# Loading keys' weight in four pieces and x tile by tile, with a new order of work, in a linear-attention block

## The chip, the cores and the metric

The kernel runs on one core of a Trainium2 chip. The metric is the device time of one execution in microseconds. Three runs of the kernel before took 169.29, 169.65 and 170.04 us; the median is 169.65.

## The reference

x has 2048 rows of 512 numbers in bf16. The block is a pre-normalized linear attention with 32 heads of 16 columns, followed by a pre-normalized dense layer with 1792 hidden columns, each with a residual:

```python
qkv = layernorm(x) @ wqkv                       # q, k, v: 32 heads of 16
phi = lambda t: where(t > 0, t + 1, exp(t)) + 1e-6
kv  = einsum("bhsd,bhse->bhde", phi(k), v)
z   = einsum("bhsd->bhd", phi(k))
o   = (phi(q) @ kv) / (phi(q) . z + 1e-6)
h   = x + o @ wo
out = h + relu(layernorm(h) @ w1) @ w2
```

## The kernel before

The 2048 rows are 16 tiles of 128 rows, and four chunks of four tiles. The program holds no loop over the work: a list of words, `ORDER` (line 18), is read from left to right (lines 539 to 542), and each word calls one small function with the numbers that follow it. The order of the words is the order of each engine's own queue. Nothing else plans the work. Each engine runs its queue in order, and an instruction waits for the data and the buffers that it needs. The landing of a DMA is signalled on one of eight semaphores, which the DMAs of both queues take in turn (the prediction calls them marks); the issue of a DMA whose semaphore is in use waits on its queue until the DMA eight places before it has landed.

The words that matter here, in the order of the computation of one tile `t`:

- `lx.t.n` loads `n` tiles of x from tile `t` on SyncE's queue (line 213), `ax.t.n` the same on ScalarE's queue (line 216). A group of `n` tiles puts `n` neighbouring rows into one partition (`rows_of`, line 101), and the output is written with the same grouping. `lk`, `lq`, `lv`, `lo`, `l1` and `l2` load pieces of the weights on SyncE's queue through `load_d` (line 219); the first number is the block of 128 rows, the second the count of blocks.
- `table` loads ScalarE's function table (line 177). `const` and `masks` fill constants on DVE and POOL. `warm` runs matmuls on zeros on PE (line 230).
- `S.t` and `A.t` are the mean and variance of a tile on DVE (lines 233 and 234), `R.t.n` the inverse root on ScalarE, an Ln and an Exp (lines 239 and 240), `N.t` the normalization on DVE (line 247). `N.t.k.n` does only `n` of the four blocks of columns.
- `T.t.b` transposes the tile on PE into bank `b` (line 272), and `E.t` copies it to SBUF on ScalarE (line 282). `X.t` transposes by a DMA on SyncE's queue instead (line 293). Both give `lnT`, the input of the products. Tiles 0 to 4 go through PE, the others through the DMA.
- `K.t.b` is the product with keys' weight, four matmuls of 512 columns, into bank `b` (line 301); `K.t.b.k.n` does only `n` of the four. `Q.c.j.b` is the product with queries' weight for a chunk (line 309).
- `F` and `U` are an exp and a relu on ScalarE, `M` and `D` a minimum and an add on DVE; together they are phi. `qF`, `qU`, `qM` and `qD` are the same for queries.
- `G.t` collects phi(k) times the normalized tile in banks 4 to 7 on PE (line 353); `gA` and `gD` copy the result on ScalarE and DVE. `z*`, `kv`, `kx`, `m`, `mA` and `mD` make the small matrices of the attention from it.
- `d4`, `dl4`, `dx4` give the reciprocal of the denominator; `wb` writes it to DRAM and `rb` (eight of them for a chunk, line 456) reads it back repeated over the columns of a head; `dm` multiplies it into phi(q) (line 469).
- `h.t.b` is the attention's output product (line 478), `hD` adds x, `s`, `a`, `r`, `n` or `nA` normalize again, and `t` with `v`, or the DMA transpose `x`, turn the tile.
- `p.c.f.b` is the first dense product (line 493; `ph` is half of it, line 502), with `pA` on ScalarE or `pD` on DVE for the relu (lines 509 and 513). `f.t.b` is the second dense product (line 522), `fo` scales and adds on DVE (line 530), into one of four output buffers (tile modulo four), and `fd` stores it (line 537).

PSUM has eight banks. A product that writes a bank waits until the instruction that reads the bank's former content is done.

The loads stand at the head of the list. ScalarE issues tiles 1 and 2 and then loads its table. SyncE issues tile 0, the whole of keys' weight, tile 3, tiles 4 and 5, tiles 6 and 7, queries' weight, tiles 8 to 11 and tiles 12 to 15. Tile 0 is normalized, transposed and copied in two halves. The output's buffers `o_t` are those of `gT`, so a store shows as `gT` in the profile, and `x_nat` is x.

Of the kernel before, what the change touches and what calls it, by code (L numbers as in the profile page):

```python
# [23 lines left out]
K.5.7 M.3.1 A.12 A.8 A.9 S.13 S.11 qU.0.0.2 X.6 qF.0.0.2 Q.0.2.0 D.2.1 A.11 K.6.2 A.13 X.7 U.4.2 F.4.2 R.8.2
qM.0.0.2 D.3.1 K.7.3 N.9 M.4.2 N.8 D.4.2 S.14 R.12.2 R.10.2 N.13 A.14 S.15 qF.0.2.2 X.9 N.10 A.15 G.0 G.2 G.1
N.12 G.3 G.4 G.5 X.8 F.6.2 U.6.2 X.13 K.9.3 R.14.2 qU.0.2.2 K.8.2 N.11 M.6.2 qD.0.0.2 D.6.2 N.15 N.14 F.8.2
U.8.2 K.13.1 X.12 X.11 qM.0.2.2 K.12.0 za.4.1 M.8.2 F.12.2 U.12.2 X.10 qD.0.2.2 G.7 K.11.3 X.14 K.10.2 G.6 D.8.2
za.6.0 X.15 K.14.0 F.10.2 M.12.2 lv.2.2 U.10.2 K.15.1 za.8.0 M.10.2 G.9 lv.0.2 zf D.10.2 G.8 zhi D.12.2 F.14.2
G.10 M.14.2 zlo G.12 U.14.2 D.14.2 z.3.3 z.0.3 z.1.3 z.2.3 zc zh G.14 d4.0.3 G.11 G.15 G.13 dl4.0 dx4.0 lo.0.2
gA.0.2 Q.1.1.3 Q.1.0.2 qF.1.0.2 lo.2.2 gD.2.2 kv.1.7 kv.2.7 kv.3.7 kv.0.7 qU.1.0.2 Q.1.3.1 qM.1.0.2 kx qD.1.0.2  # L30
Q.1.2.0 l1.0.2 m.3.7 m.2.6 mD.2.2 wb.0 rb.0.7 rb.0.3 rb.0.0 rb.0.6 rb.0.4 qF.1.2.2 qU.1.2.2 qM.1.2.2 Q.2.1.5
m.1.3 m.0.2 mA.0.2 rb.0.1 rb.0.2 Q.2.0.4 Q.2.3.1 Q.2.2.0 qF.2.0.2 qU.2.0.2 qD.1.2.2 rb.0.5 dm.0.2.2 dm.0.0.2
h.1.6 l1.2.2 d4.1.5 qF.2.2.2 qM.2.0.2 h.0.4 hD.1 dl4.1 s.1 dx4.1 a.1 hD.0 nA.1 s.0 a.0 n.0 Q.3.0.2 l2.0.7 h.2.5
hD.2 s.2 qU.2.2.2 Q.3.1.3 qU.3.0.2 wb.1 x.1 h.3.7 a.2 Q.3.3.6 hD.3 qF.3.0.2 n.2 Q.3.2.5 t.2.0 x.0 ph.0.3.1.0 s.3
a.3 n.3 ph.0.1.3.0 t.3.7 ph.0.0.2.0 rb.1.1 v.2 qM.2.2.2 r.0.4 rb.1.2 rb.1.5 qF.3.2.2 v.3 qM.3.0.2 qM.3.2.2
ph.0.2.0.0 ph.0.2.0.1 rb.1.7 ph.0.3.1.1 qD.2.0.2 qD.3.0.2 ph.0.0.2.1 qU.3.2.2 qD.3.2.2 qD.2.2.2 ph.0.1.3.1
p.0.9.5 p.0.8.4 pA.0.2.2 rb.1.3 rb.1.4 rb.1.6 d4.2.6.2 rb.1.0 dm.1.0.2 l2.7.7 dm.1.2.2 h.4.1 pD.0.0.2 dl4.2
dl4.3 dx4.2 wb.2 rb.2.6 hD.4 s.4 h.5.6 h.7.7 rb.2.7 hD.5 h.6.0 a.4 rb.2.0 rb.2.3 rb.2.4 pA.0.8.2 hD.7 hD.6 s.5
s.6 p.0.7.6 a.5 rb.2.1 p.0.6.5 p.0.4.2 p.0.5.3 s.7 a.6 a.7 p.0.13.1 rb.2.2 rb.2.5 n.4 n.7 n.5 n.6 pD.0.4.2
pD.0.6.2 p.0.11.4 p.0.12.0 dm.2.2.2 dm.2.0.2 dx4.3 p.0.10.3 pD.0.10.2 pD.0.12.2 wb.3 rb.3.4 f.2.6.0.7 rb.3.0  # L40
h.10.5 hD.10 x.6 h.9.4 hD.9 rb.3.2 rb.3.7 h.8.2 s.10 hD.8 a.10 h.11.0 s.9 s.8 rb.3.1 rb.3.6 rb.3.5 rb.3.3 hD.11
a.9 a.8 s.11 n.8 a.11 n.9 f.2.6.7.7 x.7 f.1.7.0.7 f.0.2.0.7 f.0.2.7.7 dm.3.0.2 n.10 n.11 dm.3.2.2 fo.2 fo.0
h.15.3 hD.15 x.5 x.4 x.11 h.12.4 h.13.0 s.15 hD.12 h.14.2 hD.13 a.15 s.12 f.3.3.0.7 x.10 r.4.4 p.1.0.1 hD.14
a.12 s.13 x.9 r.8.4 f.3.3.7.7 s.14 a.13 a.14 p.1.11.6 n.13 n.14 n.15 p.1.10.5 x.8 n.12 fo.3 pD.1.10.2 p.1.1.2
pD.1.0.2 f.1.7.7.7 fd.3 r.12.4 fo.1 p.1.6.3 fd.1 x.14 fd.2 p.1.7.4 p.1.3.1 p.1.4.6 p.1.5.7 p.1.2.0 pD.1.6.2
p.1.13.3 p.1.12.2 pD.1.4.2 pD.1.2.2 x.15 fd.0 x.12 pD.1.12.2 p.2.8.5 p.2.9.6 p.2.6.3 p.2.7.4 p.1.8.1 p.1.9.2
pD.2.8.2 pD.2.6.2 p.2.10.4 p.2.11.5 pD.1.8.2 pD.2.10.2 f.7.6.0.7 f.7.6.7.7 fo.7 p.2.0.4 p.2.1.5 f.4.0.0.7
f.4.0.7.7 x.13 pD.2.0.2 fo.4 f.6.1.0.7 fd.7 f.6.1.7.7 fo.6 f.5.3.0.7 f.5.3.7.7 p.3.4.5 p.3.5.6 fo.5 p.3.11.4
p.3.10.3 p.3.9.1 p.3.8.0 pD.3.4.2 p.3.6.5 p.3.7.6 pD.3.10.2 pD.3.8.2 pD.3.6.2 p.3.0.2 p.3.1.3 pD.3.0.2 p.3.3.1
p.3.2.0 pD.3.2.2 p.3.12.5 p.3.13.6 fd.4 fd.6 p.2.5.3 pD.3.12.2 f.15.4.0.14.3.1 fo.15.3.1 f.15.5.0.14.0.2  # L50
fo.15.0.2 fd.5 p.2.4.2 pD.2.4.2 p.2.3.1 p.2.2.0 p.2.12.6 pD.2.2.2 p.2.13.7 pD.2.12.2 f.8.1.0.7 f.8.1.7.7 fo.8
fd.8 f.12.4.0.7 f.12.4.7.7 fo.12 f.10.7.0.7 f.10.7.7.7 fo.10 f.13.6.0.7 fd.12 fd.10 fd.15.0.2 f.13.6.7.7 fo.13
fd.15.3.1 f.11.0.0.7 f.11.0.7.7 fo.11 fd.13 fd.11 f.14.3.0.7 f.14.3.7.7 fo.14 fd.14 f.9.0.0.7 f.9.0.7.7 fo.9
# [5 lines left out]
def kernel(  # L59
# [157 lines left out]

    def load_d(dst, src, k, n):
        nc.sync.dma_start(out=dst[:, k : k + n, :], in_=src[:, k : k + n, :])
# [353 lines left out]
```

## Time and profile before

| | |
|---|---|
| median of three runs | 169.65 us |
| profiled execution | 169.61 us |
| its span, from the first to the last instruction | 167.9 us |
| PE busy | 162.2 us |
| DVE busy | 115.8 us |
| ScalarE (ACT) busy | 49.9 us |
| bytes moved by DMA | 16.01 MB |

The profile is one execution. Times in it count from the start of the span. A row of the timeline or of the chain gives the start, the duration, the engine, the line of the kernel and the operation, `xN` for N neighbours that are merged; square brackets give the idle time before it and what ended that. PE is the matrix unit, PEld its weight loads, DVE VectorE, ACT ScalarE, POOL GpSimd, SPq and ACTq the issue of a DMA from SyncE's and ScalarE's queue. A merged row of matmuls lasts a little longer than its share of the stream, since matmuls overlap; the chain's rows give the stream.

### The profile page before, as it was taken

How to read it: one execution, taken by the hardware profiler on the slowest of the kernel's cores; microseconds unless marked ns; L12 is line 12 of the kernel's file. 1: busy time of each engine (PE TensorE's matmuls, PEld its weight loads, DVE VectorE, ACT ScalarE, POOL GpSimd, SP SyncE). 2: the span in 40 equal slices, each digit the busy share in tenths (PEclk: the TensorE clock that was granted, in tenths of full speed). 3: DMA queues.
4: the chain of work that ended last, by engine and by line, in shares of the span. 5: the costliest groups of instructions: out<-in, count | busy, mean ns of one | idle time of the engine just before them, and what ended most of it. 6: DMA issues, size and time to landing. Idle time of an engine off the chain costs nothing.

```text
span 167.9 us, 2399 instructions
## 1 busy us (share of the span) xinstructions
PE 162.2 (97%) x908; PEld 79.5 (47%) x924; DVE 115.8 (69%) x218; ACT 49.9 (30%) x84; POOL 4.7 (3%) x21
## 2 busy tenths in 40 slices
PE   7899999999999999999999999999999999999992
...
PEclk9999999999999999999999999999999999999999
...
GB/s 147 372 234 96 18 106 95 186 315 37 131 341 157 106 228 72 147 43 118 106 94 31 31 89 132 2 0 31 31 66 0 0 0 0 0 66 55 31 62 39
DMA packets 25003, 16.01 MB, mean 95 GB/s; under 512 B 15008, under 2 KB 23968, under 8 KB 24992
## 3 DMA queue, kind: packets, MB, share of 16 engines
...
q8 instruction: 7, 0.11, 0.3%
...
## 4 chain that ended last, share of the span: by engine, by line
PE 93%; DVE 2%; DMA 2%; issue 1%
PE bk L522 29%; PE bk L493 26%; PE bk L478 8%; PE bk L301 8%; PE bk L353 8%; PE bk L309 8%; PE bk L502 2%; DMA x_nat<-in_A_x_dram 2%; DVE st L233 1%; PE bk L272 1%; PE bk L425 1%; DVE gT L530 1%; PE bk L377 1%; PE bk L399 1%; PE bk L411 1%
## 5 line engine op out<-in xcount | busy, mean ns | idle before, releaser
L522 PE MATMUL bk<-w_sb,at 128*128 128x512 bf16 (+2 forms) x250 | 49.8, 355 | 0.2
L493 PE MATMUL bk<-lnT,w_sb 128*128 128x512 bf16 x200 | 45.5, 379 | 0.3
L513 DVE TENSOR_SCALAR at<-bk 128x1024 bf16<-128x1024 f32 x26 | 31.4, 1222 | 11.8 <-PE bk L493 9.4
L522 PEld LDWEIGHTS <-at 128*128 128x128 bf16 x252 | 23.6, 98 | 25.4
L493 PEld LDWEIGHTS <-w_sb 128*128 128x128 bf16 x208 | 20.3, 98 | 24.1
L530 DVE SCALAR_TENSOR_TENSOR gT<-bk,rstd,h_nat 128x512 bf16<-128x512 f32 (+2 forms) x18 | 12.4, 691 | 25.5 <-PE bk L522 25.2
L319 ACT ACTIVATE eb<-bk 128x1024 bf16<-128x1024 f32 (+1 forms) x18 | 16.6, 937 | 4.3 <-PE bk L309 1.8
L322 ACT ACTIVATE rb<-bk 128x1024 bf16<-128x1024 f32 (+1 forms) x18 | 16.5, 933 | 0.6 <-PE bk L309 0.6
L301 PE MATMUL bk<-wk_sb,lnT 128*128 128x512 bf16 x62 | 15.4, 380 | 0.1
L309 PE MATMUL bk<-lnT,wq_sb 128*128 128x512 bf16 x62 | 15.3, 379 | 0.1
L478 PE MATMUL bk<-m_sb,pqs 128*128 128x512 bf16 x64 | 15.0, 379 | 0.0
L353 PE MATMUL bk<-at,h_nat 128*128 128x512 bf16 x55 | 13.0, 379 | 0.1
L239 ACT ACTIVATE rstd<-mv,eps 128x2 f32<-128x2 f32 (+2 forms) x14 | 4.2, 298 | 27.1 <-DVE mv L236 24.6
L233 DVE BATCH_NORM_STATS2 st<-x_nat 128x6 f32<-128x512 bf16 x16 | 10.5, 676 | 2.4 <-DMA x_nat<-in_A_x_dram 2.4
L484 DVE TENSOR_TENSOR h_nat<-bk,x_nat 128x512 bf16<-128x512 f32 x16 | 10.7, 679 | 1.0 <-PE bk L478 0.9
L235 DVE BATCH_NORM_STATS2 st<-h_nat 128x6 f32<-128x512 bf16 x16 | 10.6, 680 | 0.2
L478 PEld LDWEIGHTS <-pqs 128*128 128x128 bf16 x64 | 6.1, 98 | 7.8 <-issue 0.7
L309 PEld LDWEIGHTS <-wq_sb 128*128 128x128 bf16 x64 | 6.2, 98 | 7.3
L353 PEld LDWEIGHTS <-h_nat 128*128 128x128 bf16 x64 | 6.1, 98 | 7.3 <-issue 0.2
L301 PEld LDWEIGHTS <-lnT 128*128 128x128 bf16 x64 | 5.8, 98 | 6.8 <-DMA lnT<-h_nat 0.6
L326 DVE TENSOR_SCALAR eb<-eb 128x1024 bf16<-128x1024 bf16 (+1 forms) x18 | 6.8, 388 | 1.6 <-ACT eb L319 1.6
L247 DVE TENSOR_SCALAR h_nat<-x_nat,mv,rstd 128x512 bf16<-128x512 bf16 (+1 forms) x17 | 6.5, 396 | 0.2
...
## 6 DMA issues: line engine op xcount, KB each, us to landing
...
out_dram<-gT SPq DMA_DIRECT2D x15, 128.0 KB, 1.9
x_nat<-in_A_x_dram SPq DMA_DIRECT2D x2, 512.0 KB, 7.7
wk_sb<-in_A_wqkv_dram SPq DMA_DIRECT2D x1, 512.0 KB, 4.6
...
wq_sb<-in_A_wqkv_dram SPq DMA_DIRECT2D x1, 512.0 KB, 6.5
...
```

Of the source, the lines that this page charges most:

```text
L233: op_S = lambda t: nc.vector.bn_stats(out=st[:, t, :], in_=x_nat[:, t, :])
L301: nc.tensor.matmul(bk[:, b, :], lhsT=lnT[c][:, kd, j * P : (j + 1) * P], rhs=wk_sb[:, kd, :], start=(kd == 0), stop=(kd == KD - 1),)
L309: nc.tensor.matmul(bk[:, b, :], lhsT=wq_sb[:, kd, j * P : (j + 1) * P], rhs=lnT[c][:, kd, :], start=(kd == 0), stop=(kd == KD - 1),)
L319: nc.scalar.activation(out=buf(eb, kind, i, n), in_=bank(at_bank[kind, i], n), func=ACT.Exp)
L322: nc.scalar.activation(out=buf(rb, kind, i, n), in_=bank(at_bank[kind, i], n), func=ACT.Relu)
L353: nc.tensor.matmul(bk[:, KD + kd, :], lhsT=ln_nat[:, t, kd * P : (kd + 1) * P], rhs=pk(t)[:, 0, :], start=(not stated), stop=(len(stated) ...
L478: nc.tensor.matmul(bk[:, b, :], lhsT=pqs[:, (c * KD + jb) % NQ, j * P : (j + 1) * P], rhs=m_sb[:, jb, :], start=(jb == 0), stop=(jb == KD ...
L484: nc.vector.tensor_tensor(out=h_nat[:, t : t + n, :], in0=bank(at_bank["h", t], n), in1=x_nat[:, t : t + n, :], op=ALU.add,)
L493: nc.tensor.matmul(bk[:, b, :], lhsT=w1_sb[:, kd, f * P : (f + 1) * P], rhs=lnT[c][:, kd, :], start=(kd == 0), stop=(kd == KD - 1),)
L513: nc.vector.tensor_scalar(out=acts[c % 2][:, f : f + n, :], in0=bank(at_bank["p", c, f], n), scalar1=-1.0, scalar2=0.0, op0=ALU.mult, op1= ...
L522: nc.tensor.matmul(bk[:, b, 0 : w * P], lhsT=acts[c % 2][:, f, j * P : (j + 1) * P], rhs=w2_sb[:, f, k * P : (k + w) * P], start=(f == 0), ...
L530: nc.vector.scalar_tensor_tensor(out=o_t[:, t % NO, cols], in0=bk[:, at_bank["f", t, k], 0 : w * P], scalar=rstd2[:, t : t + 1], in1=h_nat ...
```

## The change

The loads at the head of the list are dealt out anew, and the list behind them is a new order of nearly the same words.

- Keys' weight comes in four loads of 128 KB: blocks 0 and 2 on SyncE's queue (`lk.0.1`, `lk.2.1`), blocks 1 and 3 on ScalarE's (`ak.1.1`, `ak.3.1`, a new function).
- ScalarE loads its table first, then issues blocks 1 and 3 and tile 3 (`ax.3.1`). It no longer issues tiles 1 and 2.
- SyncE issues tiles 0, 1 and 2 one by one, then blocks 0 and 2 of the weight, tiles 4 and 5, tiles 6 and 7, queries' weight, and tiles 8 to 15 as one load of 1 MB (`lx.8.8`). With that the rows of tiles 8 to 15 are grouped by eight instead of by four.
- Tile 0 is normalized, transposed and copied whole (`N.0`, `T.0.4`, `E.0`). K.0 is whole; K.1, K.2 and K.3 stay in halves.
- Behind that the same products run in another order, many in other banks. `gA` and `gD` exchange their halves, and so do `mA` and `mD`. `n.0` becomes `nA.0`. Of the pairs of the first chunk's `p`, ScalarE takes pair 0 alone, where it had pairs 2 and 8. `Q.1.1` stands ahead of the `z` products instead of behind `gA`.

The diff, cut to the head and the parts that the prediction speaks of:

```diff
-ax.1.1 ax.2.1 table const masks warm.70.7.64 warm.2.7 lx.0.1 S.0 A.0 S.1 lk.0.4 R.0.1 N.0.0.2 lx.3.1 A.1 S.2
-R.1.1 lx.4.2 T.0.3.0.2 N.0.2.2 A.2 E.0.0.2 R.2.1 T.0.2.2.2 E.0.2.2 lx.6.2 N.1 lq.0.4 K.0.5.0.2 T.1.3 S.3 lx.8.4
-K.0.5.2.2 N.2 E.1 A.3 R.3.1 lx.12.4 T.2.6 E.2 S.5 N.3 S.4 K.1.0.0.2 A.5 F.0.1 K.1.0.2.2 T.3.3 E.3 K.2.2.0.2
-K.2.2.2.2 A.4 S.7 K.3.3.0.2 Q.0.3.1 R.4.2 U.0.1 F.1.1 S.6 F.2.1 N.4 T.4.6 K.3.3.2.2 A.6 A.7 R.6.2 N.5 M.1.1
+table ak.1.1 ak.3.1 ax.3.1 const masks warm.70.7.64 warm.2.7 lx.0.1 S.0 A.0 lx.1.1 lx.2.1 S.1 lk.0.1 lk.2.1 A.1
+R.0.1 R.1.1 N.0 T.0.4 E.0 S.2 N.1 lx.4.2 A.2 lx.6.2 S.3 R.2.1 N.2 T.1.2 E.1 A.3 K.0.5 T.2.0 R.3.1 S.5 K.1.2.0.2
+K.1.2.2.2 N.3 E.2 S.4 A.5 F.0.1 T.3.3 A.4 E.3 lq.0.4 S.7 S.6 A.7 A.6 R.4.2 F.1.1 M.1.1 N.5 U.1.1 lx.8.8 R.6.2
+K.2.6.0.2 K.2.6.2.2 N.4 K.3.7.0.2 Q.0.3.1 Q.0.1.3 U.0.1 U.2.1 N.7 N.6 M.0.1 T.4.4 K.3.7.2.2 E.4 S.8 Q.0.0.2
...
+N.13 R.10.2 S.15 S.14 N.11 F.6.2 U.6.2 G.2 G.0 G.1 A.14 X.9 X.8 G.4 G.3 G.5 X.13 A.15 N.10 N.12 qF.0.2.2 X.12
...
+D.12.2 lv.2.2 za.8.0 U.10.2 M.10.2 Q.1.1.3 F.14.2 zf D.10.2 zhi lv.0.2 G.9 G.11 G.10 U.14.2 lo.0.2 zlo M.14.2
...
+m.1.3 m.2.6 m.3.7 qU.1.2.2 mA.2.2 Q.2.0.4 qD.1.0.2 qM.1.2.2 rb.0.0 mD.0.2 qD.1.2.2 rb.0.6 rb.0.3 rb.0.7 rb.0.5
...
+p.0.6.4 pD.0.2.2 rb.1.3 l2.7.7 dm.1.0.2 dl4.2 dx4.2 wb.2 dm.1.2.2 h.7.6 pD.0.6.2 h.4.2 hD.7 hD.4 h.6.4 h.5.3
...
+p.1.3.3 p.1.2.2 fo.3 p.1.12.5 p.1.13.6 pD.1.4.2 p.1.10.0 x.9 x.8 x.14 fd.1 p.1.11.1 f.2.7.0.7 pD.1.2.2 pD.1.12.2
...
+fo.14 fd.14 fd.11 fd.12 fd.13 f.10.6.7.7 fo.10 f.15.7.0.14.2.1 fd.10 fo.15.2.1 fd.15.2.1
...
+    def op_ak(k, n):
+        nc.scalar.dma_start(out=wk_sb[:, k : k + n, :], in_=wqkv_v[:, k : k + n, D : 2 * D])
+
```

More of the change, by code (lines that the diff above doesn't have):

```diff
@@ L24 @@
[L24 to L53, printed above, removed]
@@ L54 @@
-fd.9 f.15.6.0.14.2.1 fo.15.2.1 fd.15.2.1
+table ak.1.1 ak.3.1 ax.3.1 const masks warm.70.7.64 warm.2.7 lx.0.1 S.0 A.0 lx.1.1 lx.2.1 S.1 lk.0.1 lk.2.1 A.1
+R.0.1 R.1.1 N.0 T.0.4 E.0 S.2 N.1 lx.4.2 A.2 lx.6.2 S.3 R.2.1 N.2 T.1.2 E.1 A.3 K.0.5 T.2.0 R.3.1 S.5 K.1.2.0.2
+K.1.2.2.2 N.3 E.2 S.4 A.5 F.0.1 T.3.3 A.4 E.3 lq.0.4 S.7 S.6 A.7 A.6 R.4.2 F.1.1 M.1.1 N.5 U.1.1 lx.8.8 R.6.2
+K.2.6.0.2 K.2.6.2.2 N.4 K.3.7.0.2 Q.0.3.1 Q.0.1.3 U.0.1 U.2.1 N.7 N.6 M.0.1 T.4.4 K.3.7.2.2 E.4 S.8 Q.0.0.2
+K.4.5 F.2.1 U.3.1 D.0.1 D.1.1 qU.0.0.2 qF.0.0.2 X.5 K.5.6 A.8 S.13 S.9 F.4.2 Q.0.2.0 A.13 M.2.1 U.4.2 F.3.1 A.9
@@ new lines @@
+S.10 qM.0.0.2 D.2.1 A.10 S.12 X.6 X.7 M.4.2 R.8.2 A.12 R.12.2 S.11 M.3.1 A.11 N.9 K.6.2 K.7.3 N.8 D.4.2 D.3.1
+N.13 R.10.2 S.15 S.14 N.11 F.6.2 U.6.2 G.2 G.0 G.1 A.14 X.9 X.8 G.4 G.3 G.5 X.13 A.15 N.10 N.12 qF.0.2.2 X.12
+R.14.2 X.11 K.9.3 M.6.2 K.8.2 qD.0.0.2 qU.0.2.2 K.13.1 qM.0.2.2 D.6.2 G.7 K.12.0 N.14 qD.0.2.2 za.4.1 F.8.2
+M.8.2 U.8.2 F.12.2 G.6 N.15 K.11.3 U.12.2 X.10 K.10.2 X.14 D.8.2 K.14.0 za.6.0 G.8 X.15 K.15.1 M.12.2 F.10.2
+D.12.2 lv.2.2 za.8.0 U.10.2 M.10.2 Q.1.1.3 F.14.2 zf D.10.2 zhi lv.0.2 G.9 G.11 G.10 U.14.2 lo.0.2 zlo M.14.2
@@ new lines @@
+D.14.2 z.0.2 z.3.2 z.2.2 z.1.2 zc zh lo.2.2 G.14 d4.0.2 dl4.0 G.13 G.15 G.12 dx4.0 l1.0.2 Q.1.0.2 gD.0.2 gA.2.2
+qF.1.0.2 Q.1.2.0 wb.0 rb.0.1 qM.1.0.2 kv.0.6 kv.2.6 kv.3.6 kv.1.6 kx Q.1.3.1 qU.1.0.2 Q.2.1.5 qF.1.2.2 m.0.2
+m.1.3 m.2.6 m.3.7 qU.1.2.2 mA.2.2 Q.2.0.4 qD.1.0.2 qM.1.2.2 rb.0.0 mD.0.2 qD.1.2.2 rb.0.6 rb.0.3 rb.0.7 rb.0.5
+rb.0.2 rb.0.4 dm.0.0.2 qF.2.0.2 Q.2.2.0 Q.2.3.1 qU.2.0.2 dm.0.2.2 qM.2.0.2 h.1.6 qU.2.2.2 d4.1.2 dl4.1 h.0.3
+hD.1 s.1 h.2.6 a.1 dx4.1 hD.0 s.0 l1.2.2 a.0 nA.1 l2.0.7 hD.2 h.3.7 wb.1 hD.3 s.2 qF.2.2.2 Q.3.0.3 Q.3.1.4 nA.0
```

18 lines of the change are left out of this document (17 added, 1 removed).

## The prediction

> **What bounds the kernel now.** I read the page first, then the chain of work in order of time, then the timeline of the first 14 us. The page's lines give the span, the busy times, PE's slices and the clock.
>
> ```profile
> span 167.9 us, 2399 instructions
> PE 162.2 (97%) x908; PEld 79.5 (47%) x924; DVE 115.8 (69%) x218; ACT 49.9 (30%) x84; POOL 4.7 (3%) x21
> PE   7899999999999999999999999999999999999992
> PEclk9999999999999999999999999999999999999999
> ```
>
> PE is full from the third slice on, at the full clock. The span is therefore the time at which PE becomes dense, plus its work, plus a short tail. So the chain is followed only where PE is not yet dense, and at the very end.
>
> ```profile
> 0.79 2.80 DMA x_nat<-in_A_x_dram
> ...
> 3.62 0.70 DVE st L233
> 4.34 0.18 DVE mv L234
> 5.12 0.41 DVE h_nat L247
> ...
> 8.14 0.22 PE bk L272 x4
> ...
> 10.80 0.86 PE bk L309 x4
> ...
> 164.12 0.76 DVE gT L530
> ```
>
> The start hangs on x tile 0 landing, its statistics, its normalization, then transposes and the keys' product. The 0.86 for four gives 0.216 us for one 512-column matmul; four transposes cost 0.22.
>
> ```profile
> 1.04 4.34 PE L230 MATMUL bk<-m_sb 128*128 128x64 bf16 x71 [1.04 <-DVE m_sb L185]
> 4.44 0.66 DVE L233 BATCH_NORM_STATS2 st<-x_nat 128x6 f32<-128x512 bf16 x1
> 4.56 0.29 ACT L239 ACTIVATE rstd<-mv,eps 128x1 f32<-128x1 f32 x1 [1.56 <-DVE mv L234]
> 5.60 0.42 PE L272 MATMUL bk<-ident,h_nat 128*128 128x128 bf16 x2 [0.22 <-DVE h_nat L247]
> 6.09 0.36 ACT L282 ACTIVATE lnT<-bk 128x256 bf16<-128x256 bf16 x1
> 6.56 0.38 DVE L247 TENSOR_SCALAR h_nat<-x_nat,mv,rstd 128x512 bf16<-128x512 bf16 x1
> 6.85 0.69 DVE L233 BATCH_NORM_STATS2 st<-x_nat 128x6 f32<-128x512 bf16 x1
> 7.46 0.40 DVE L247 TENSOR_SCALAR h_nat<-x_nat,mv,rstd 128x512 bf16<-128x512 bf16 x1
> 8.51 0.58 ACT L282 ACTIVATE lnT<-bk 128x512 bf16<-128x512 bf16 x1
> 10.63 1.03 PE L309 MATMUL bk<-lnT,wq_sb 128*128 128x512 bf16 x4
> ```
>
> At 10.63 the first query product starts, with 16 transposes and 14 key matmuls behind it. The changed order reaches the same point (T.0 to T.3, K.0, K.1, K.2, half of K.3, then Q.0.3), so this is the mark to compare.
>
> **The change, part by part.** *Tile 0 whole.* In the rows the first half-tile normalization takes 0.41 and a whole tile takes 0.40 (at 7.46): on the path the half saved nothing. Its second half had to wait behind the next tile's statistics. In the new order DVE runs S.0 3.62, A.0 4.34, S.1 4.44, A.1 5.16 (4.34 - 3.62 after its S), then N.0 whole at about 5.27 instead of 5.12, to 5.67. T.0 follows at 5.74 (0.07 later, as 5.53 to 5.60), E.0 at about 6.16, and its 0.58 ends at 6.74. Tile 1 sits behind: S.2 at 5.58 (a normalization occupies 0.29 to 0.31: 6.56 to 6.85), N.1 at 6.19 (6.85 to 7.46 is 0.61), T.1 about 6.64 to 6.86. K.0 then starts near 6.87, and PE has work without a gap: K.0 0.86, T.2 0.22, K.1 0.86, T.3 0.22, K.2 0.86, two of K.3 0.43, together 3.45. Q.0.3 starts at 10.32, against 10.63: a gain of 0.3. The cover is thin: N.2 must end by about 7.7, and by the same steps it ends at 7.6.
>
> *x tile 0 alone at the head of the queues.* Before, tiles 0 and 1 were issued in the same moment by SyncE and ScalarE. The DMA answers for 2 to 3 us, the second half of it, and tiles 0 and 1 to landing (least, median, most):
>
> ```profile
> q1 hardware_dynamic: 121, 0.11, 46.2%
> q10 hardware_dynamic: 120, 0.11, 33.1%
> 2.50:3.00 0.50, 0.50 (x14) 0.50 (x12) 0.00 (x0) 0.50 (x1) 0.39 (x2) 1.00 1.01 340
> DMA to landing us min/median/max: 2.8/2.9/3.0
> ```
>
> The queues moved 121 and 120 packets side by side, so tile 0 paid for tile 1. Alone, its 0.13 MB at 340 GB/s need 0.39 us of the wire, which would end it up to 0.4 earlier. If the 2.8 is latency, it gains nothing. I take 0.2, between the ends: the packets do interleave, but 0.39 of 2.8 us is little, and the rest is not the wire. The Trainium skill, page "DMA: Bandwidth & Descriptors", section "Queues, rings and completion order", says that each DMA engine takes turns between the queue rows that have work. By that rule the trace agrees (121 to 120), and the sum with the full 0.4 would be 0.2 lower than mine. The warm-up matmuls end at 5.38 (1.04 + 4.34), so T.0 could not use more than about 0.35 in any case.
>
> *Keys' weight in four loads, and ScalarE's three loads behind its table.*
>
> ```profile
> 0.79 0.90 ACTq L216 DMA_DIRECT2D x_nat<-in_A_x_dram  x2
> 1.72 1.28 ACT L177 ACT_TABLE_LOAD   x1 [1.72 <-PEq L557]
> 3.20 0.43 SPq L219 DMA_DIRECT2D wq_sb<-in_A_wqkv_dram  x1
> 3.79 0.92 SPq L213 DMA_DIRECT2D x_nat<-in_A_x_dram  x2
> x_nat<-in_A_x_dram ACTq DMA_DIRECT2D x2, 128.0 KB, 3.7
> x_nat<-in_A_x_dram SPq DMA_DIRECT2D x2, 512.0 KB, 7.7
> ```
>
> ScalarE loads its table at 0.79 instead of 1.72, to 2.07, then issues three loads at about 0.45 each (0.90 for two): 2.07, 2.52, 2.97, free at 3.43. Its next instruction, the Ln of tile 0, is wanted at 4.56 (4.36 with the 0.2): covered by 0.9. SyncE issues nine loads instead of eight before the first transposed tile, at some 0.45 each. The last piece is issued near 2.6; with the 3.7 that the 128 KB loads of ScalarE took in the median it lands at 6.3, and K.0 starts at 6.87: nothing. Tile 3 is the tight one: issued at 2.97, wanted by S.3 at about 6.5 (6.3). With the same 3.7 it lands at 6.7. Bounds 0 to 0.4 late; I charge 0.1, because the large load that shared their time is now in pieces. Queries' weight lands earlier than Q.0.3 needs by any of these rates.
>
> *Tiles 8 to 15 as one load.* Its 1 MB ends no earlier than the two 512 KB loads did: 3.79 + 0.45 + 7.7 or so, 12. S.8, the first reader, comes at about 12.3 in the new DVE order. A wait of up to 0.5 there delays N.9 and the transposed tiles, and then D.4, on which G.4 hangs at 20.2. By the steps above G.4 has some 0.5 of cover, so I charge nothing; without the cover it costs what exceeds it.
>
> *The new order behind that.* It does the same matmuls. Swaps of gA and gD and of mA and mD cost nothing, as they work side by side. n.0 goes to ScalarE (nA.0), and one p pair goes from ScalarE to DVE.
>
> ```profile
> L261 ACT ACTIVATE hn<-h_nat,mv x1: 721/721/721, 51.8 to 51.8; 128x512 bf16<-128x512 bf16 x1
> L513 DVE TENSOR_SCALAR at<-bk 128x1024 bf16<-128x1024 f32 x26 | 31.4, 1222 | 11.8 <-PE bk L493 9.4
> out_dram<-gT SPq DMA_DIRECT2D x15, 128.0 KB, 1.9
> 93.39 2.36 DVE L513 TENSOR_SCALAR at<-bk 128x1024 bf16<-128x1024 f32 x2 [0.97 <-PE bk L493]
> 49.10 1.03 PE L478 MATMUL bk<-m_sb,pqs 128*128 128x512 bf16 x4
> ```
>
> nA.0 puts 0.72 on ScalarE before x.0; the pair puts 1.22 on DVE between 60 and 77, where it works almost without a pause until the idle 0.97 ahead of 93.39. The first place where PE would notice is h.6, which takes the bank that pD.0.6 frees: I find both near 64, with no margin. Next is p.1.10, which takes the bank of pD.1.4 near 93.7, also with about 0.1. Bounds: 0 (the 0.97 absorbs it) to 1.22. I take 0.1, nearer to 0, because nearly all the pairs later on have DVE at 1.22 against 1.73 of PE (eight matmuls). z comes one Q later, since Q.1.1 now stands ahead of it, so the read-back for dm.0 lands up to 0.6 later against h.1, which started at 49.10. Bounds 0 to 0.6; DVE has as much other work ahead of dm.0 as before, and its two halves now come in the order in which h reads them: I take 0.
>
> At the end fo.10 writes the buffer that fd.14 sends away. fd.14 starts about 0.8 after f.14 ends (the 0.76 of fo.9 at 164.12) and takes 1.9: 2.7, while f.10 needs 14 x 0.216 = 3.02. Covered by 0.3.
>
> **Sum.** The profiled execution took 169.61, 1.7 more than its span and 0.04 under the median of the runs (169.65). 169.61 - 0.3 (tile 0 whole) - 0.2 (tile 0 alone) + 0.1 (tile 3) + 0.1 (DVE) = 169.3. A change under 0.5% (0.85 us) counts as none: that is about what a measurement of this kernel can tell from no change.
>
> **Rivals.** *The three loads of ScalarE come late for want of a completion mark (slower).* The loads take eight marks in turn. The trace shows the ninth holding: the issue at 3.20 ends at 3.63, and the next starts only at 3.79, which is 0.79 + 3.0, when tile 1 had landed. There are twelve loads now. If ScalarE's third is numbered behind SyncE's eighth, it waits for a weight piece, about 5.0, and R.0 stands behind it on ScalarE's queue. R.0 would then run at 5.45 instead of 4.36, N.0 1.1 later, and tile 3 would land at 5.0 + 2.8 = 7.8 instead of 6.3, which puts T.2 1.5 later. Price 1.5: 170.8. It decides from the point where that third issue ends after 4.36. Against it: by the issue times above ScalarE's third (2.97) comes before SyncE's sixth.
>
> *ScalarE is not free when its table load ends (no change).* The trace shows 1.28 and then a wait for DVE until 4.56; it can't show whether an issue could have followed at once. If the loads start 1.3 later (as long again as the load itself), tile 3 lands 1.3 later, S.3 is late by about 1.2 and T.2 by 1.0: 170.2. The Trainium skill, page "ScalarE: Activation LUTs", section "What ACT_TABLE_LOAD costs", speaks for it: it gives about 1283 ns for the load and about 1380 ns of drain behind it. By that rule the first load is issued at some 3.4; no run here shows it yet.
>
> *Only a later stage pays (slower).* If DVE's extra 1.22 reaches PE at h.6 in full, 170.4; it needs DVE to be without any slack from 60 to 77, and the 0.97 at 93.39 speaks against it.
>
> *The head gains all it can (faster).* 0.35 from tile 0 and no charge for tile 3 and DVE: 169.0, which still counts as none. A gain over 0.85 needs a second idle stretch on PE, and PE's slices show none.
>
> **How the numbers follow.** Head as forecast, within 168.9 to 169.8, the full gain included: 0.6. Late marks: 0.1. Table: 0.1. Later stage: 0.12, half of it over 170.5. A gain on PE that I don't see: 0.08. The range is 168.7 to 170.6; above it remain some of the late marks, below it most of the unseen gain. Faster 0.08; slower 0.1 + 0.06, and 0.05 of the first case from small stalls that add up, 0.21; same the rest, 0.71.
>
> **What would show it.** S.0 should start at 3.2 to 3.6; K.0's first matmul near 6.6 to 6.9 and no gap up to Q.0.3, at 10.1 to 10.4. ScalarE's three issues should end by 3.5, and the third landing before 6.5. S.8 should wait less than 0.5. DVE should still have idle time ahead of the p.1 pairs. The prediction is wrong if Q.0.3 starts after 10.7, or if PE shows idle time behind it.

## The result, and the profile after

The changed kernel takes 170.94 us in the median of 20 runs (169.82 to 171.99); the kernel before took 169.74 us in 20 runs beside it (169.29 to 171.74). The ratio is 1.0062, with a 95% interval of 1.004 to 1.0084: slower by 0.6%. The forecast was 169.3 us and no measurable change, with a range to 170.6. The time and the sign are both missed.

The runs of the changed kernel also scatter more than those of before. The profiled execution, 169.85 us with a span of 168.1, is one of its shortest. The page's span and busy times of it:

```profile
span 168.1 us, 2398 instructions
PE 161.6 (96%) x908; PEld 79.4 (47%) x924; DVE 116.2 (69%) x217; ACT 49.9 (30%) x83; POOL 4.7 (3%) x21
```

The work is that of before. What differs lies at the head, and the timeline shows it (start, duration, engine, line; the lines of the loads are one lower than before the change, those behind the new function two higher):

```profile
0.79 1.28 ACT L176 ACT_TABLE_LOAD   x1 [0.79 <-PEq L559]
0.82 0.87 ACTq L221 DMA_DIRECT2D wk_sb<-in_A_wqkv_dram  x2
1.72 0.45 ACTq L215 DMA_DIRECT2D x_nat<-in_A_x_dram  x1
...
0.80 1.34 SPq L212 DMA_DIRECT2D x_nat<-in_A_x_dram  x3
2.19 0.91 SPq L218 DMA_DIRECT2D wk_sb<-in_A_wqkv_dram  x2
3.59 0.88 SPq L212 DMA_DIRECT2D x_nat<-in_A_x_dram  x2
5.87 0.39 SPq L218 DMA_DIRECT2D wq_sb<-in_A_wqkv_dram  x1
6.31 0.51 SPq L212 DMA_DIRECT2D x_nat<-in_A_x_dram  x1
...
3.60 0.69 DVE L235 BATCH_NORM_STATS2 st<-x_nat 128x6 f32<-128x512 bf16 x1 [2.36 <-DMA x_nat<-in_A_x_dram]
5.88 0.69 DVE L235 BATCH_NORM_STATS2 st<-x_nat 128x6 f32<-128x512 bf16 x1 [0.27 <-DMA x_nat<-in_A_x_dram]
12.88 0.69 DVE L235 BATCH_NORM_STATS2 st<-x_nat 128x6 f32<-128x512 bf16 x1
...
6.95 0.40 PE L274 MATMUL bk<-ident,h_nat 128*128 128x128 bf16 x4 [0.88 <-DVE h_nat L249]
7.18 1.03 PE L303 MATMUL bk<-wk_sb,lnT 128*128 128x512 bf16 x4
10.68 1.67 PE L311 MATMUL bk<-lnT,wq_sb 128*128 128x512 bf16 x7
```

Three things are to be seen. ScalarE's loads are not behind its table load but during it: the first two go out from 0.82, tile 3 at 1.72. Tile 2 is waited for at 5.88, so T.1 comes at 6.95, K.0 at 7.18 and Q.0.3 at 10.68 (10.63 before). And SyncE's queue stands still, above all in two places: tiles 4 and 5 are issued from 3.59, and queries' weight, which was issued at 3.20 before, at 5.87. Tiles 8 to 15 follow at 6.31. SyncE's waits up to 12 us say for what:

```profile
SPq L218 <- DMA x_nat<-in_A_x_dram: 1.4, 1, 1.4
SPq L212 <- DMA x_nat<-in_A_x_dram: 0.7, 2, 0.5
```

The weight's load needs no data of x. It waits because the semaphore that it is to signal on is still that of tile 2 (the trace has number 104 for both), eight loads earlier in the order in which the semaphores are dealt out. That order is close to the order of issue, but not the same: by issue, the third load is a piece of the weight. The chain shows when that load landed:

```profile
1.72 4.14 DMA x_nat<-in_A_x_dram
5.86 0.02 issue
5.88 0.04 DVE st L235
```

The issues of DMAs give the large load 6.5 us to landing:

```profile
x_nat<-in_A_x_dram SPq DMA_DIRECT2D x1, 1024.0 KB, 6.5
```

So tiles 8 to 15 landed at 6.31 + 6.5 = 12.8, and S.8 started at 12.88. In this execution that is just in time. The wire shows the hold too: the windows from 7 to 8 and from 10 to 12 us, first of the kernel before, then of the changed one (the last two columns are the DMA's busy share and GB/s):

```profile
7.00:8.00 1.00, 1.00 (x9) 0.50 (x8) 1.00 (x4) 0.89 (x3) 0.00 (x0) 1.00 1.10 365
...
10.00:11.00 1.00, 1.00 (x6) 0.41 (x5) 1.00 (x3) 0.97 (x5) 0.00 (x0) 1.00 0.83 320
11.00:12.00 1.00, 1.00 (x10) 0.57 (x8) 1.00 (x7) 1.00 (x4) 0.00 (x0) 1.00 0.04 16
```

```profile
7.00:8.00 1.00, 1.00 (x8) 0.48 (x8) 0.98 (x4) 0.96 (x3) 0.00 (x0) 1.00 0.68 145
...
10.00:11.00 1.00, 1.00 (x6) 0.41 (x5) 1.00 (x3) 0.97 (x5) 0.00 (x0) 1.00 1.00 426
11.00:12.00 1.00, 1.00 (x7) 0.42 (x5) 1.00 (x6) 0.97 (x5) 0.00 (x0) 1.00 0.61 246
```

Before, the DMA engines were full up to 10 and all but done at 11, with the last landing at 12.3. After, the wire runs half empty at 7 to 8 (145 GB/s against 365), since nothing new had been issued between 4.5 and 5.87, and the same bytes end near 12.

### The profile page after: what moved, and what is told of

It is laid out like the page before. It is cut to its first block, busy times and chain, and to the rows that moved or that the text cites. A ratio compares the mean times of both kernels' runs of the same rounds, so it can differ in the third digit from the quotient of the medians.

```text
span 168.1 us, 2398 instructions
## 1 busy us (share of the span) xinstructions
PE 161.6 (96%) x908; PEld 79.4 (47%) x924; DVE 116.2 (69%) x217; ACT 49.9 (30%) x83; POOL 4.7 (3%) x21
## 4 chain that ended last, share of the span: by engine, by line
PE 93%; DMA 2%; issue 1%; SPq 0%; DVE 0%
PE bk L524 29%; PE bk L495 27%; PE bk L480 8%; PE bk L311 8%; PE bk L355 8%; PE bk L303 8%; DMA x_nat<-in_A_x_dram 2%; PE bk L504 2%; PE bk L274 1%; PE bk L427 1%; PE bk L379 1%; PE bk L401 1%; PE bk L413 1%; SPq L212 0%; DVE h_nat L249 0%
## 5 line engine op out<-in xcount | busy, mean ns | idle before, releaser
L515 DVE TENSOR_SCALAR at<-bk 128x1024 bf16<-128x1024 f32 x27 | 32.8, 1223 | 12.0 <-PE bk L495 11.4
L532 DVE SCALAR_TENSOR_TENSOR gT<-bk,rstd,h_nat 128x512 bf16<-128x512 f32 (+2 forms) x18 | 12.4, 692 | 25.5 <-PE bk L524 25.4
L321 ACT ACTIVATE eb<-bk 128x1024 bf16<-128x1024 f32 (+1 forms) x18 | 16.6, 928 | 4.6 <-PE bk L303 2.0
L324 ACT ACTIVATE rb<-bk 128x1024 bf16<-128x1024 f32 (+1 forms) x18 | 16.4, 930 | 0.0
L355 PE MATMUL bk<-at,h_nat 128*128 128x512 bf16 x54 | 13.1, 379 | 0.2 <-issue 0.2
L235 DVE BATCH_NORM_STATS2 st<-x_nat 128x6 f32<-128x512 bf16 x16 | 10.5, 672 | 2.6 <-DMA x_nat<-in_A_x_dram 2.6
L486 DVE TENSOR_TENSOR h_nat<-bk,x_nat 128x512 bf16<-128x512 f32 x16 | 10.5, 675 | 0.5 <-PE bk L480 0.4
L249 DVE TENSOR_SCALAR h_nat<-x_nat,mv,rstd 128x512 bf16<-128x512 bf16 x16 | 6.1, 405 | 0.1
```

Source lines behind the costliest of these rows:

```text
L235: op_S = lambda t: nc.vector.bn_stats(out=st[:, t, :], in_=x_nat[:, t, :])
L321: nc.scalar.activation(out=buf(eb, kind, i, n), in_=bank(at_bank[kind, i], n), func=ACT.Exp)
L324: nc.scalar.activation(out=buf(rb, kind, i, n), in_=bank(at_bank[kind, i], n), func=ACT.Relu)
L355: nc.tensor.matmul(bk[:, KD + kd, :], lhsT=ln_nat[:, t, kd * P : (kd + 1) * P], rhs=pk(t)[:, 0, :], start=(not stated), stop=(len(stated) ...
L486: nc.vector.tensor_tensor(out=h_nat[:, t : t + n, :], in0=bank(at_bank["h", t], n), in1=x_nat[:, t : t + n, :], op=ALU.add,)
L515: nc.vector.tensor_scalar(out=acts[c % 2][:, f : f + n, :], in0=bank(at_bank["p", c, f], n), scalar1=-1.0, scalar2=0.0, op0=ALU.mult, op1= ...
```

## The experiments

The kernels differ in the deal of the early loads and in which order follows them. All count the loads ahead of values' weight; the changed kernel has twelve, the kernel before ten.

**First group: is it the loads or the order?** The theories on record: H, the head (tile 2 lands late and variably, because ScalarE issues during its table load); L, the load of 1 MB lands late as such; O, the new order has stalls of its own. The kernel before took 169.98 us beside these four.

*The old order with the new loads.*

```diff
-ax.1.1 ax.2.1 table ... lx.0.1 S.0 A.0 S.1 lk.0.4 R.0.1 N.0.0.2 lx.3.1 ... lx.8.4 ... lx.12.4
+table ak.1.1 ak.3.1 ax.3.1 ... lx.0.1 S.0 A.0 lx.1.1 lx.2.1 S.1 lk.0.1 lk.2.1 R.0.1 N.0.0.2 ... lx.8.8
```

> Old order of the work, new loads at its head (four weight pieces, tile 3 on ScalarE, tiles 1 and 2 on SyncE, tiles 8 to 15 in one load). Theory H (head: tile 2 lands late and by a varying amount, since ScalarE issues its three loads while its table is still loading): about as slow as the changed kernel, 170.3 to 171.2, with a spread of over 1 us, and S.2 waiting for tile 2 until 5.8 or later. Theory L (the one load of 1 MB lands late): 170 to 171 too. Theory O (the new order behind the head has stalls of its own): 169.7, like the kernel before.

Measured: 171.22 us, ratio 1.0068 (1.0044 to 1.0092). In the profiled execution tile 2 landed at 5.56, a little earlier than H had said, and S.10, the first reader of the large load in this order, waited for it 1.69 us, until 13.87.

*The new order with the old loads.* The reverse edit, in the changed kernel.

> New order of the work, old loads at its head. Theory H: 169.3 to 169.6, with the small spread of the kernel before, and Q.0.3 starting near 10.4 to 10.7. Theory L: 169.5 as well. Theory O: 170.5 to 171.

Measured: 169.55 us, ratio 0.9985 (0.996 to 1.001). The timeline has T.1, K.0 and Q.0.3 at:

```profile
6.53 0.40 PE L274 MATMUL bk<-ident,h_nat 128*128 128x128 bf16 x4 [0.37 <-DVE h_nat L249]
6.84 1.04 PE L303 MATMUL bk<-wk_sb,lnT 128*128 128x512 bf16 x4
...
10.34 1.89 PE L311 MATMUL bk<-lnT,wq_sb 128*128 128x512 bf16 x8
```

The two runs settle it: the new loads cost about the same in either order, 0.7% in the old (1.0068) and 0.8% in the new (1.0062 against 0.9985), and the new order alone costs nothing. O is out. With the old loads Q.0.3 starts at 10.34, near the 10.32 of the prediction's step for tile 0; S.0 started at 3.47 here, though, and not at the 3.62 of that working.

*The changed kernel with tiles 8 to 15 in two loads again.*

```diff
-lx.8.8
+lx.8.4 lx.12.4
```

> The changed kernel with tiles 8 to 15 in two loads of 512 KB again. Theory H: unchanged, 170.6 to 171.1. Theory L: S.8 no longer waits, 169.7. Theory O: unchanged, 170.9.

Measured: 170.82 us, ratio 1.0053 (1.0029 to 1.0077). Splitting the load repairs nothing, so L is out. The chain of this execution names another victim, queries' weight, issued when tile 2 had landed, and Q.0.3 behind it:

```profile
1.72 4.05 DMA x_nat<-in_A_x_dram
...
5.78 5.01 DMA wq_sb<-in_A_wqkv_dram
...
10.84 1.90 PE bk L312 x8
```

*All of keys' weight and tile 3 on SyncE, none on ScalarE.*

```diff
-table ak.1.1 ak.3.1 ax.3.1 ... lk.0.1 lk.2.1
+table ... lk.0.1 lk.1.1 lk.2.1 lk.3.1 lx.3.1
```

> The changed kernel with all four weight pieces and tile 3 on SyncE's queue behind tiles 0 to 2; ScalarE issues no load. Theory H: tile 2 lands near 4.6 to 5.0, K.0 starts near 6.9, Q.0.3 near 10.4, 169.2 to 169.5 with a small spread, unless the last weight piece becomes the one that is late. Theories L and O: unchanged, 170.9.

Measured: 171.39 us, ratio 1.007 (1.0045 to 1.0094), slower than the changed kernel, although ScalarE issued nothing. From its timeline:

```profile
2.85 0.69 DVE L235 BATCH_NORM_STATS2 st<-x_nat 128x6 f32<-128x512 bf16 x1 [1.60 <-DMA x_nat<-in_A_x_dram]
...
18.13 1.24 PE L303 MATMUL bk<-wk_sb,lnT 128*128 128x512 bf16 x5 [0.95 <-ACT eb L321]
```

Tile 0, with nothing on the other queue, was there at 2.85 (3.60 in the changed kernel), and tile 2 at 3.91. It gave nothing in the end: tiles 8 to 15 were issued at 5.99, landed 8.66 later, and K.6 waited 0.95 at 18.13. H, as the reason that the end is late, is out too. The run has two effects of its own. Tile 3, now the eighth load on one queue, landed at 7.05 and S.3 waited 1.01 for it, the next tiles 0.41, so that Q.0.3 came at 11.18, 0.84 behind the run with the old loads. And no issue was held here: SyncE's twelve loads follow each other every 0.45 to 0.5 us, which alone puts the last one at 5.99. What the slow ones of these kernels share is twelve loads and more, and late issues of the last ones.

**Second group: the weight ahead of the tiles, or the count of loads?** Theory W: pieces of keys' weight go ahead of tile 2 on the wire. Theory M: twelve loads on eight semaphores hold back the last ones. The kernel before took 169.85 us.

*Twelve loads, but tiles 1 and 2 first.*

```diff
-table ak.1.1 ak.3.1 ax.3.1 ... lx.0.1 S.0 A.0 lx.1.1 lx.2.1 S.1 lk.0.1 lk.2.1
+ax.1.1 ax.2.1 table ak.1.1 ... lx.0.1 S.0 A.0 lk.0.1 lk.2.1 S.1 lk.3.1 lx.3.1
```

> The changed kernel with its twelve loads, but with tiles 1 and 2 first on ScalarE's queue (as before the change) and three of the four pieces of keys' weight on SyncE behind tile 0, one on ScalarE behind its table load. Theory W (the pieces of keys' weight go ahead of tile 2 and share the wire with it): tile 2 lands by 4.6 us, S.2 and S.3 wait for nothing, Q.0.3 starts at 10.3 to 10.5, and the time returns to 169.6 (169.3 to 169.9). Theory M (twelve loads on eight marks: queries' weight and tiles 8 to 15 are issued only when early loads have landed): queries' weight is issued at 4.8 us or later, tiles 8 to 15 after it and landing later than 12, and the time stays at 170.5 to 171.2 although tile 2 is early.

Measured: 170.45 us, ratio 1.0038 (1.0017 to 1.006). Tile 2 was early, S.2 and S.3 waited for nothing, Q.0.3 started at 10.54, and the kernel stayed slow: tiles 8 to 15 were issued at 5.00 and took 9.20, and K.6 waited 0.83 at 17.69. W explains at most part of it. M had put the issue of queries' weight at 4.8 or later; it was at 4.53, and the median is just under M's 170.5. The 9.20 us of the large load are more than the late issue explains; the second execution of the changed kernel, below, shows what stretches it.

*Keys' weight in two loads: ten loads.*

```diff
-table ak.1.1 ak.3.1 ax.3.1 ... lk.0.1 lk.2.1
+table ak.2.2 ax.3.1 ... lk.0.2
```

> The changed kernel with keys' weight in two loads of 256 KB (one per queue) instead of four of 128 KB: ten loads ahead of wv's instead of twelve. Theory M: queries' weight is the ninth load and is issued by about 4.2 us (5.87 in the changed kernel), tiles 8 to 15 by 4.7 (6.31); they land by 9.5 and 11.5; the time falls to 169.6 to 169.9. Theory W: half of the weight still goes ahead of tiles 1 and 2, tile 2 lands at 5.5 to 6, and the time stays at 170.5 to 171.2.

Measured: 169.71 us, ratio 1.0005 (0.9978 to 1.0031). Half of the weight is still issued ahead of tile 2, which landed at 5.22, and the loss is gone. Queries' weight was issued at 3.64, tiles 8 to 15 at 4.52, as M had said; they landed later than its 9.5 and 11.5, at 9.9 and 12.4. The time is M's and not W's.

*The new order and the old loads, with only tiles 8 to 15 as one load: nine loads.*

```diff
-table ak.1.1 ak.3.1 ax.3.1 ... lx.0.1 S.0 A.0 lx.1.1 lx.2.1 S.1 lk.0.1 lk.2.1
+ax.1.1 ax.2.1 table ... lx.0.1 S.0 A.0 S.1 lk.0.4 lx.3.1
```

> The new order with the old deal of the early loads (tiles 1 and 2 on ScalarE ahead of its table load, keys' weight in one load), and of the new loads only the one for tiles 8 to 15. Theories W and M both: ten loads or fewer and the weight behind the tiles, so as with all the old loads, 169.55 (169.3 to 169.8). Theory L (a load of 1 MB lands late as such): tiles 8 to 15 land at 12.3 or later, S.8 waits, and the time is 170.2 or more.

Measured: 169.44 us, ratio 0.9969 (0.9955 to 0.9982). The large load is harmless, and this kernel is faster than both.

*The changed kernel again,* a second profiled execution:

> The changed kernel unaltered, for a second profiled execution, since its times lie between 169.8 and 172.0. Theory M: a longer execution shows queries' weight landing after 10.3 us or tiles 8 to 15 after 12.8, and PE waiting for them (Q.0.3, or K.6 behind the transposed tiles). Theory W: it shows tile 2 landing later than 5.86, and the first key products with it. A third reading: the extra time lies behind 20 us, in which case neither holds.

It took 170.52 us, near the median, and shows where the usual loss lies. Its chain:

```profile
1.72 3.82 DMA x_nat<-in_A_x_dram
5.54 0.02 issue
5.56 0.39 SPq L218
5.95 0.04 issue
5.99 7.74 DMA x_nat<-in_A_x_dram
...
13.75 0.04 DVE st L235
13.79 0.58 issue
14.36 0.76 DVE pk_lo L331 x2
...
15.23 1.02 ACT rb L324
16.25 0.92 ACT eb L321
...
17.21 1.89 PE bk L303 x8
```

Read downwards: tile 2 lands, the issue of queries' weight and then of tiles 8 to 15 may follow, the large load lands at 13.73, S.8 starts at 13.75. Behind S.8 on DVE's queue stand D.0 and D.1 (L331). They free the buffers for `qU` (L324), `qF` (L321) comes behind it on ScalarE and frees the banks of K.6, and K.6 starts at 17.21, after an idle time of PE of 0.73. From there on PE is dense. The first of the G products starts at 19.10, where the new order with the old loads had 18.06: 1.04 of the 1.30 us between the two executions' times (170.52 and 169.22).

What stretches the large load stands in the packets of this trace. Beside the loads, the first 16 us hold one transfer of 16 KB in a queue that the profile calls `instruction`:

```profile
q8 instruction: 1, 0.02, 0.4%
```

It ran from 11.47 to 12.44. Of the large load's 128 packets of 8 KB all but one were over by 11.94. The last started at 12.43, took 0.80 us where the others took 0.31, and the landing followed at 13.73. The two runs with the longest loads show the same: all on SyncE, the 16 KB from 11.71 to 12.74 and the next packet at 12.73; tiles first, 11.63 to 12.60 and 12.59. The traces don't say which of the 16 DMA engines moved a packet, so that these stood behind the 16 KB on the same engine is inferred from the times. In the first execution of the changed kernel the transfer ran from 11.61 to 12.63, but the load's last packet was over at 12.33, and it landed at 12.76. With nine loads the packets were over at 11.27 and 11.52, before the transfer ended (11.84 and 11.61). So the late issue leaves part of the load to move when this transfer comes, and whether a packet is caught behind it makes about 1 us of difference.

**Third group: the count of loads by itself.** Theory M as above; theory P: the pieces of weight ahead of the tiles. The added loads move 32 bytes each into a buffer that nothing reads, so the output is unchanged. The kernel before took 169.88 us.

*Three tiny loads in front, twelve loads.* The edit is made in the nine-load kernel:

```diff
-ax.1.1 ax.2.1 table
+ax.1.1 ax.2.1 ap.0 ap.1 ap.2 table
...
+    op_ap = lambda i: nc.scalar.dma_start(out=pad[0:1, 16 * i : 16 * i + 16], in_=wqkv_v[0:1, 0, 0:16])
```

> The new order with the old deal of early loads and tiles 8 to 15 in one load (nine loads, 169.44 us), and three more loads of 32 bytes each, into a buffer that nothing reads, on ScalarE's queue behind tiles 1 and 2: twelve loads again, as in the changed kernel, with the bytes and their order untouched. Theory M (the count of loads on eight marks is what costs): queries' weight is issued at 4.2 us or later instead of 3.26, tiles 8 to 15 at 5 to 6 instead of 3.73, they land at 12.8 or later, S.8 waits, and the time is 170.1 to 170.8. Theory P (the weight in pieces ahead of the tiles costs, not the count): nothing moves, 169.4 to 169.6.

Measured: 170.56 us; against the kernel before 1.0027 (0.9999 to 1.0056), against the same kernel without the tiny loads beside it (169.37, highest 169.69) 1.2 us more, with ten of the twelve runs above that highest. Hardly a byte was added. In the profiled execution SyncE's queue and the wire look like those of the changed kernel; first the issues of the two last loads, then the window from 7 to 8:

```profile
5.46 0.38 SPq L219 DMA_DIRECT2D wq_sb<-in_A_wqkv_dram  x1
6.01 0.37 SPq L213 DMA_DIRECT2D x_nat<-in_A_x_dram  x1
```

```profile
7.00:8.00 1.00, 1.00 (x9) 0.44 (x8) 0.93 (x4) 0.88 (x4) 0.00 (x0) 1.00 0.64 132
```

The landing came at 6.01 + 6.8 = 12.8, as M said, but in this one execution S.8 did not have to wait for it, and PE's gap lay elsewhere, 0.68 us at 73.81, behind the read-back of the second chunk's reciprocals. That left a doubt, which the fourth group takes up. The packets name a likely cause: another 16 KB `instruction` transfer ran from 69.98 to 71.75, no packet of the read-back moved between 70.92 and 71.74, and the last twelve ended at 72.69. That gap is evidence for neither theory.

*Keys' weight in two, and two tiny loads, twelve again.* The edit is made in the ten-load kernel:

```diff
-table ak.2.2 ax.3.1
+table ak.2.2 ax.3.1 ap.0 ap.1
```

> The changed kernel with keys' weight in two loads (ten loads, 169.71 us) and two more loads of 32 bytes each, into a buffer that nothing reads, on ScalarE's queue behind tile 3: twelve loads again. Theory M: queries' weight is issued at 5 us or later instead of 3.64, tiles 8 to 15 land at 12.8 or later, and the time is 170.3 to 171.0. Theory P: 169.6 to 169.9, as without them.

Measured: 170.73 us (lowest 169.86), ratio 1.0028 (1.0004 to 1.0052), where the same deal with ten loads took 169.71. Queries' weight was issued at 5.50 and tiles 8 to 15 at 5.92, landing 7.13 later at 13.05. K.7 waited at 18.46 for its transposed tile, from which the chain leads back through DVE's D to the landing of tiles 8 to 15:

```profile
18.46 1.04 PE L305 MATMUL bk<-wk_sb,lnT 128*128 128x512 bf16 x4 [0.79 <-DMA lnT<-h_nat]
```

Both kernels with tiny loads meet M in their times and refute P. The wait that M put ahead of PE shows in the second of them alone.

*The nine-load kernel once more.*

> The new order with the old deal of early loads and tiles 8 to 15 in one load, once more, as the best version so far and beside the two kernels with tiny loads: 169.3 to 169.6, and faster than the kernel before by 0.1 to 0.4%.

Measured: 169.37 us (169.19 to 169.69), ratio 0.9972 (0.996 to 0.9984).

**Fourth group: the hold, or the shift?** Each added load also shifts which semaphore every later transfer takes. Theory S: that shift costs, not the hold. The kernel before took 169.97 us.

*The three tiny loads behind the 1 MB load.*

```diff
-lx.8.8
+lx.8.8 ap.0 ap.1 ap.2
...
+    op_ap = lambda i: nc.sync.dma_start(out=pad[0:1, 16 * i : 16 * i + 16], in_=wqkv_v[0:1, 0, 0:16])
```

> The new order with the old deal of early loads and tiles 8 to 15 in one load (169.37 to 169.44 us), and the three loads of 32 bytes on SyncE behind the load of tiles 8 to 15 instead of on ScalarE ahead of it. All later transfers take marks shifted by three, as with the tiny loads in front, but nothing is held at the head: queries' weight is issued at 3.2 to 3.3 us, tiles 8 to 15 at 3.7 to 3.9. Theory M (the hold at the head): 169.3 to 169.6. Theory S (the shift of the marks for later transfers): 170.2 to 170.8, as with the tiny loads in front.

Measured: 169.76 us, ratio 0.9986 (0.9973 to 0.9999). The issues are back at 3.23 and 3.71, and the landing is at 11.6. The hold was most of the loss. The time is 0.2 above what M had given, so a small part may belong to the shift or to the three issues themselves; the runs don't tell. The three loads also changed their queue here, from ScalarE's to SyncE's, so place and queue were not told apart.

*The kernel with tiny loads in front, a second profiled execution.*

> The kernel with three tiny loads in front, once more, for a second profiled execution. Theory M: tiles 8 to 15 land at 12.8 us or later, and if the span is near 169, S.8 waits for them and PE has its gap before 21 us. Theory S: the gap is again near 73.8, with the read-back of the reciprocals late.

It took 169.68 us with no gap of PE at all: queries' weight issued at 4.35, tiles 8 to 15 at 5.80, landing at 12.4, and S.8 at 12.77. This answers neither theory, since the execution was a short one. M's landing of 12.8 or later did not come true here.

*The changed kernel, a third profiled execution.*

> The changed kernel, for a third profiled execution. Theory M: a span above 168.4 goes with a landing of tiles 8 to 15 after 12.9 us and a gap of PE before 21 us of about the difference. Theory S: the gap lies behind 21 us.

It took 170.12 us (span 168.4). DVE's and PE's rows:

```profile
13.12 0.69 DVE L235 BATCH_NORM_STATS2 st<-x_nat 128x6 f32<-128x512 bf16 x1 [0.56 <-DMA x_nat<-in_A_x_dram]
...
16.59 1.89 PE L303 MATMUL bk<-wk_sb,lnT 128*128 128x512 bf16 x8 [0.32 <-ACT eb L321]
```

S.8 at 13.12 and a gap of 0.32, S.8 at 13.75 and a gap of 0.73, S.8 at 12.88 and none: in the three executions of the changed kernel the gap ahead of K.6 follows the landing of tiles 8 to 15. M is half met: the landing is at 13.1, but the gap is a third of the 0.9 us between this span and the 167.5 of the new order with the old loads. PE fell 0.30 further behind at 57.22, after 21 us, and the profile doesn't say for what.

The deals side by side, from the profiled executions (the landing is the issue plus the time to landing; all on SyncE, the issues are late without a hold):

| deal of the early loads | loads | queries' weight issued | tiles 8 to 15 issued / landed | median |
|---|---|---|---|---|
| nine loads, two profiles | 9 | 3.26, 3.20 | 3.73 / 11.8, 3.84 / 11.9 | 169.44, 169.37 |
| weight in two | 10 | 3.64 | 4.52 / 12.4 | 169.71 |
| weight in two, two tiny | 12 | 5.50 | 5.92 / 13.05 | 170.73 |
| nine, three tiny in front, two profiles | 12 | 5.46, 4.35 | 6.01 / 12.8, 5.80 / 12.4 | 170.56 |
| tiles first | 12 | 4.53 | 5.00 / 14.2 | 170.45 |
| changed kernel, three profiles | 12 | 5.87, 5.56, 5.14 | 6.31 / 12.8, 5.99 / 13.7, 5.58 / 13.1 | 170.94 |
| all on SyncE | 12 | 5.51 | 5.99 / 14.65 | 171.39 |
| nine, three tiny behind | 9 + 3 | 3.23 | 3.71 / 11.6 | 169.76 |

## Why the prediction was wrong

**The step that failed** is *Tiles 8 to 15 as one load*, with the sentence on queries' weight ahead of it. It took the issue at 3.79 from the kernel before, added 0.45 and 7.7, and got 12, against S.8 at 12.3; for queries' weight it said "earlier than Q.0.3 needs by any of these rates". The duration was fair (6.5, 7.74 and 7.5 us in the three executions). The issue was not: 6.31, 5.99 and 5.58. The prediction had the means to see it. It had read in the trace that the issue of the ninth load held until a landing, and counted twelve loads in the rival of the late marks, but followed them only to ScalarE's third load. Numbered through, the ninth to twelfth are tiles 4 and 5, tiles 6 and 7, queries' weight and tiles 8 to 15, all on SyncE. By the semaphores in the trace the eleventh waits for tile 2, whose landing the prediction never timed. The twelfth has the semaphore of a piece of weight that had landed at 3.76, but it stands behind the eleventh on the queue. So the semaphore rival had the right mechanism and the wrong load: ScalarE's third went out at 1.72 without a wait.

The same step had the wrong way from S.8 to PE. It gave G.4 half a microsecond of cover, and called nothing what K.6 then paid. What stands right behind S.8 on DVE's queue is D.0 and D.1, and by way of ScalarE they carry the wait to K.6 with little cover: 0.97 of wait became 0.73 on PE (second execution), 0.56 became 0.32 (third).

**Tile 0 whole, -0.3: the right way, half the size.** With the old loads Q.0.3 is at 10.34 against the 10.32 of the working, but that agreement is luck, since S.0 started 0.15 earlier than in the working. From S.0 to Q.0.3 it took 7.01 us before and 6.76 to 6.87 in the seven profiled executions of the new order in which neither an early tile nor queries' weight was waited for; the working had 6.70. The gain is 0.14 to 0.25. In the changed kernel the late tile 2 took it back (10.68), and the statement that Q.0.3 comes at 10.1 to 10.4 failed there, as did K.0 by 6.9 (7.18).

**Tile 0 alone at the head, -0.2: wrong in its premise.** Tile 0 was not alone, since ScalarE's pieces of weight were issued from 0.82. S.0 started at 3.60, within the 3.2 to 3.6 named and without a gain on 3.62. Where nothing stood on the other queue, S.0 came at 2.85, 0.75 earlier. The landings behind these starts are 2.82 there and 3.25 to 3.58 in five executions with pieces of weight on the other queue, so the bound of 0.4 from the wire time was too small. The Trainium skill's rule of turns between queue rows ("DMA: Bandwidth & Descriptors", section "Queues, rings and completion order") agrees with the starts at 2.85 and 3.60.

**ScalarE's loads at 2.07, 2.52 and 2.97: wrong.** The first two were issued from 0.82 to 1.69 and the third at 1.72, while the table loaded from 0.79 to 2.07. The rival that ScalarE isn't free when its table load ends had no place either. The 1380 ns of drain that the Trainium skill gives ("ScalarE: Activation LUTs", section "What ACT_TABLE_LOAD costs") doesn't show in these issues, and the first Ln comes at 4.55, too late to tell.

**Tile 3 late, +0.1.** S.3 followed S.2 without a wait for it (6.89 in the changed kernel): nothing. The tile to charge was tile 2, with 0.27 of wait at 5.88 and a later T.1 (6.95 against 6.64 in the working).

**DVE's extra pair, +0.1, and the new order.** PE shows no wait for the pairs of the first dense product from 60 to 97 us, and DVE still sat idle for 0.50 at 96.25. Nothing to charge; the 0.97 of idle time took it up. The new order alone ran at 0.9985 of before, so the rival of the later stage is out.

**The account.** The old loads with the new order give 169.55, against the 169.3 forecast. The starts of the same matmul in two traces say where a kernel falls behind; the measure here is the profiled execution of the new order with the old loads (169.22).

- First execution (169.85): 0.42 late from T.1 on, for want of tile 2, and 0.43 at the last matmul. Tiles 8 to 15 cost nothing.
- Second (170.52): 0.15 at Q.0.3, 1.04 from K.6 on (the gap is 0.73 of it), 1.10 at the last matmul, and some 0.2 behind that, at the store.
- Third (170.12): 0.02 up to K.6, 0.41 behind it, and 0.70 from 57.22 on.

So the late tile 2 cost 0 to 0.42 and the late tiles 8 to 15 0 to 0.9, and the same loads lose their time at different places from one execution to the next. The median (170.94) lies 0.42 above the slowest of the three. The longest runs, up to 171.99, were not caught in a profile of the changed kernel; that in them the landing is later still, as the 14.2 and 14.65 of two other deals suggest, is argued and not shown. When the 16 KB transfer comes, and why, is open as well.
